# Contiguous-row weight transfers and an earlier first dV in a memory-bound transformer-block backward kernel

## Chip, cores, metric

One core of a Trainium2 chip. The metric is the device time of one execution in microseconds (us), as the median of several executions.

## What is computed

Forward and backward of a decode block: layer norm, attention of one query against a K and V cache, output projection, then layer norm and a gated MLP, and the gradients of everything.

```python
# x (4,1,512), k_cache and v_cache (4,32,4096,128), wq (512,4096), wo (4096,512)
# w1, w3 (512,1792), w2 (1792,512); all bf16
def _A_ref(x, k_cache, v_cache, wq, wo):
    q = heads(x @ wq)
    p = softmax(einsum("bhqd,bhkd->bhqk", q, k_cache) * Dh ** -0.5)
    return merge(einsum("bhqk,bhkd->bhqd", p, v_cache)) @ wo
h  = x + _A_ref(layernorm(x), ...)
h2 = h + (silu(n @ w1) * (n @ w3)) @ w2          # n = layernorm(h)
# reference returns h2 and the gradients of x, k_cache, v_cache, wq, wo, w1, w3, w2
```

K, V, dK and dV are 134 MB each, and V is read twice (once for the output, once for dP). So 705 MB must move and hardly anything else matters: dV of a head is an outer product of the softmax row P and dO, dK one of dS and q.

## The kernel before

The program has three parts: the forward over 128 heads (K and V in, no writes), the **middle** (MLP forward and backward on 4 rows, ending in dO), and the backward over 128 heads (V in, dK and dV out). SBUF is a ring of 23 slots of about 1 MB. Weight loads and weight gradients of the second half are **side work**, cut into pieces by `yield` and fed in between the heads.

```python
    class Slot:                                    # one of 23 buffers [128, 4160] bf16
        def __init__(self, name, src=free):
            self.i = src.popleft()                 # in order of giving back; waits until its last use is done
            ...
    def load_w2():
        sl = two_slots("w2")
        for i in range(2):
            nc.sync.dma_start(out=sl[i].b(7 * D).rearrange("p (c j) -> p c j", c=7),
                              in_=B_w2[i * 7 * P:(i + 1) * 7 * P, :].rearrange("(c p) j -> p c j", p=P))
    ...
    # end of the middle: dO of head 0 of all four batch rows spread to 128 partitions
    ps = psA.tile([P, B, Dh], FP32, tag="rT", name="rep_ps")
    for b in range(B):
        for jj in range(DC):
            nc.tensor.matmul(ps[:, b, :], lhsT=dhT[:, jj, b:b + 1].to_broadcast([P, P]), rhs=wo_page(0)[:, 0, jj, :], ...)
    nc.scalar.copy(out=rep_bufs["rdo"][0], in_=ps[:])
    dO_columns(0, 8, psC, "cols")                  # dO of 8 heads as columns, for dP
    mid_w["wo"][0].give()
    V_T(0, psT, range(2, SJ // GW))                # rest of V of head 0 transposed
    ...
    # side work: second load of wq, by blocks of columns, 2 KB rows
    nc.sync.dma_start(out=wq2s[-1].b(DC * HH * Dh).rearrange("p (c n) -> p c n", c=DC),
                      in_=A_wq[:, ch * HH * Dh:(ch + 1) * HH * Dh].rearrange("(c p) n -> p c n", p=P))
    ...
    # gradient of wo, 1 KB rows (those of w2 likewise)
    nc.gpsimd.dma_start(out=out_5[h0 * P:(h0 + 8) * P, :].rearrange("(h p) j -> p h j", p=P),
                        in_=st.b(8 * D).rearrange("p (h j) -> p h j", h=8))
    ...
    O0, S0 = 2, 18                                 # heads at which dO pages and side work start
    P_pairs(0); P_pairs(1)
    grad_V(0)                                      # outer product on DVE, then a GpSimd DMA
    dO_rows(0, 8, psg, "gps")
    front(0)                                       # transposes V, dP = V dO; P_pairs(s+2) on GpSimd
    for s in range(NH):
        prefetch()
        if s + 1 < NH:
            ...
            front(s + 1)
            grad_V(s + 1)
        grad_K(s)
        ...
```

## Time and profile before

| | before |
|---|---|
| median of 4 runs | 1732.17 us (1729.33 to 1736.33) |
| span of the profiled run | 1729.8 us |
| moved | 707.86 MB, 409 GB/s |
| busy: PE, DVE, ACT, GpSimd | 77%, 72%, 55%, 25% |
| packets of weight reads from SP's queue | 7680 of 1024 bytes, 2048 of 2048, 1024 of 3584 |
| packets of weight writes from GpSimd's queue | 1472 of 4096 bytes, 512 of 7168 |

One thing helps in all that follows: the DMA engines are busy nearly throughout, so progress is best measured in bytes moved, and two traces of this program are best compared at **equal bytes**. I took the packet records of each trace, added up the sizes in order of their ends (without instruction fetches), and noted when 20, 280, 330, 470, 580 and 690 MB had landed. The forward ends near 280 MB, the middle and its after-effects lie at 280 to 330, the weight loads of the second half (wq, then w2) at 470 to 580, the weight gradient writes of w2, w1/w3 and wo at 580 to 690.

### The profile page before, as it was taken

What the parts mean: (1) busy time and instruction counts of PE and PEld (TensorE: products, weight loads), DVE (VectorE), ACT (ScalarE), POOL (GpSimd) and SP (SyncE); (2) the same over time, 40 slices, a digit from 0 to 9 for tenths busy, and PEclk for the clock granted to TensorE, in tenths of its full rate; (3) what the DMA queues carried; (4) which work ended last, traced back from release to release, by engine and by line L of the source; (5) the groups of instructions that cost most, each with busy time, mean ns of one, the idle gap of its engine ahead of it and who ended that gap; (6) DMA issues with size and microseconds to landing.
All of it is one profiled execution on the core that took longest, in us unless ns stands there. A gap on an engine that the chain in (4) does not pass through costs nothing.

```text
span 1729.8 us, 44048 instructions
## 1 busy us (share of the span) xinstructions
PE 1328.0 (77%) x19014; PEld 1121.1 (65%) x19014; DVE 1253.1 (72%) x1388; ACT 959.0 (55%) x1469; POOL 432.5 (25%) x808
## 2 busy tenths in 40 slices
PE   5888888888888888867788777875776867777662
PEld 4667666777666666866677777765654655556562
DVE  5989899889998996576657666665557555555773
ACT  3455445444454444666655555555665767667562
POOL 1211232223222321222212312232123223212331
PEclk8999999999999999666655565556775656555555
DMA  9999999999999999899999999999999999999997
GB/s 399 410 418 418 419 418 419 418 418 417 415 417 408 418 402 391 342 392 424 418 416 412 413 411 414 414 413 418 422 423 421 425 419 411 412 413 411 407 417 294
DMA packets 107179, 707.86 MB, mean 409 GB/s; under 512 B 11284, under 2 KB 18976, under 8 KB 24040
## 3 DMA queue, kind: packets, MB, share of 16 engines
q1 hardware_dynamic: 66880, 422.60, 59.4%
q0 software_dynamic: 39712, 282.37, 39.9%
q8 instruction: 149, 2.44, 0.5%
q14 instruction: 46, 0.38, 0.1%
q10 hardware_dynamic: 392, 0.07, 0.0%
HBM read 422.59 MB, written 282.34 MB: 408 GB/s over the span
## 4 chain that ended last, share of the span: by engine, by line
DMA 38%; PE 8%; ACT 7%; DVE 6%; issue 3%; ACTq 0%; POOL 0%; DVEq 0%; POOLq 0%
DMA out_dram<-gk 22%; DMA out_dram<-gv 9%; ACT VT L760 5%; DMA wq<-in_A_wq_dram 3%; DVE gk L1116 3%; PE pt_tps L759 3%; DVE gv L1116 2%; DMA out_dram<-gwq 2%; DMA out_dram<-gw 1%; PE gps L909 1%; PE M_ps L433 1%; DVE PK L418 1%; PE dP_ps L1110 1%; PE pt_w L562 0%; PE rep_ps L1088 0%
## 5 line engine op out<-in xcount | busy, mean ns | idle before, releaser
L760 ACT COPY VT<-pt_tps 128x1024 bf16<-128x1024 bf16 x512 | 493.1, 1016 | 231.0 <-PE pt_tps L759 122.2
L759 PE MATMUL pt_tps<-ident_b,V 128*128 128x128 bf16 x4096 | 455.2, 294 | 112.7 <-ACT VT L760 98.1
L759 PEld LDWEIGHTS <-V 128*128 128x128 bf16 x4096 | 404.1, 138 | 183.9 <-issue 161.1
L1116 DVE TENSOR_TENSOR gv<-P,reps 128x4096 bf16<-128x4096 bf16 x128 | 293.2, 2291 | 241.2 <-DMA out_dram<-gk 117.5
L1116 DVE TENSOR_TENSOR gk<-dS,reps 128x4096 bf16<-128x4096 bf16 x128 | 293.4, 2292 | 64.4 <-DMA out_dram<-gv 33.0
L433 PE MATMUL M_ps<-PK,Vn 128*128 128x130 bf16 x4096 | 285.7, 222 | 51.5 <-DMA Vn<-in_A_v_cache_dram 50.9
L418 DVE TENSOR_TENSOR PK<-Kn,PK 128x4096 bf16<-128x4096 bf16 x128 | 292.3, 2283 | 32.5 <-POOL PK L414 32.2
L433 PEld LDWEIGHTS <-Vn 128*128 128x128 bf16 x4096 | 252.4, 99 | 73.2 <-DMA Vn<-in_A_v_cache_dram 67.6
L325 DVE STREAM_TRANSPOSE KT<-Kn 128x512 f32<-128x512 f32 (+1 forms) x321 | 250.6, 797 | 0.3 <-issue 0.2
L320 ACT COPY KT<-pt_tps 128x1024 bf16<-128x1024 bf16 x128 | 129.5, 1012 | 193.1 <-PE pt_tps L319 153.1
L1110 PE MATMUL dP_ps<-dOT_bf,VT 128*128 128x1 bf16 x4096 | 152.8, 166 | 67.0 <-ACT VT L760 66.0
L1110 PEld LDWEIGHTS <-VT 128*128 128x128 bf16 x4096 | 140.4, 103 | 79.8 <-ACT VT L760 78.5
L1141 POOL DMA_DIRECT2D out_dram<-gk x128 | 68.1, 532 | 358.5 <-DVE gk L1116 257.5
L1127 POOL DMA_DIRECT2D out_dram<-gv x128 | 68.5, 535 | 322.6 <-DVE dSt L1134 241.7
L331 POOL TENSOR_TENSOR W<-qrep,wmask 128x128 bf16<-128x128 bf16 x128 | 123.9, 968 | 82.2 <-PE S_ps L351 67.4
L414 POOL COPY PK<-P_all 128x64 bf16<-128x64 bf16 x128 | 32.4, 253 | 421.9 <-ACT P_all L408 418.8
L1100 POOL COPY P<-P_all 128x64 bf16<-128x64 bf16 x128 | 112.0, 876 | 0.0
L408 ACT COPY P_all<-pt_P 32x64 bf16<-32x64 bf16 x256 | 51.9, 203 | 59.8 <-PE pt_P L404 57.6
L319 PE MATMUL pt_tps<-ident_b,Kn 128*128 128x128 bf16 x1024 | 80.7, 224 | 0.0
L443 PE MATMUL kP_ps<-PK,onesw 128*32 128x512 bf16 x1024 | 79.2, 386 | 0.0
L319 PEld LDWEIGHTS <-Kn 128*128 128x128 bf16 x1024 | 62.0, 100 | 25.9 <-issue 25.8
L397 ACT ACTIVATE Pn<-E,rl 128x1024 bf16<-128x1024 f32 x64 | 73.7, 1152 | 3.2 <-DVE rl L394 3.2
(228 smaller groups left out, 1294.0 us busy)
## 6 DMA issues: line engine op xcount, KB each, us to landing
Kn<-in_A_k_cache_dram SPq DMA_DIRECT2D x128, 1024.0 KB, 15.6
Vn<-in_A_v_cache_dram SPq DMA_DIRECT2D x128, 1024.0 KB, 16.0
V<-in_A_v_cache_dram SPq DMA_DIRECT2D x128, 1024.0 KB, 11.0
out_dram<-gv POOLq DMA_DIRECT2D x128, 1024.0 KB, 24.6
out_dram<-gk POOLq DMA_DIRECT2D x128, 1024.0 KB, 25.1
wq<-in_A_wq_dram SPq DMA_DIRECT2D x8, 1024.0 KB, 11.2
out_dram<-gw POOLq DMA_DIRECT2D x6, 896.0 KB, 27.4
wo<-in_A_wo_dram SPq DMA_DIRECT2D x4, 1024.0 KB, 13.3
```

Source lines behind the costliest of these rows:

```text
L319: nc.tensor.transpose(pt[:, i, :], Kn[:, c * GW + i, :], ident_b[:])
L320: nc.scalar.copy(out=KT[:, c * GW:(c + 1) * GW, :], in_=pt[:])
L325: nc.vector.transpose(out=KT[:, c * w_:(c + n) * w_], in_=Kn[:, c * w_:(c + n) * w_])
L331: nc.gpsimd.tensor_tensor(out=W[:, hl], in0=qrep[:, :, s:s + 1].to_broadcast([P, 4, 32]), in1=wmask[:, hl, None, :].to_broadcast([P, 4, 32 ...
L418: nc.vector.tensor_tensor(out=PK[:, :, 0:Dh].rearrange("p j (r t) -> p j r t", t=2), in0=Ks[s].heads().rearrange("p j (r t) -> p j r t", t=2),
L433: nc.tensor.matmul(hold["M"][:], lhsT=Vn[:, j, :], rhs=PK[:, j, :], start=(j == 0), stop=(j == SJ - 1))
L443: nc.tensor.matmul(hold["kP"][32 * q:32 * (q + 1), :, :], lhsT=ones_window(w), rhs=PK[:, j0:j0 + 4, 0:Dh], start=(w == 0 and c == 0), stop ...
L759: nc.tensor.transpose(pt[:, i, :], Vn[:, g * GW + i, :], ident_b[:])
L760: nc.scalar.copy(out=VT[:, g * GW:(g + 1) * GW, :], in_=pt[:])
L1100: nc.gpsimd.tensor_copy(out=P2s[s][:], in_=P_all[:, s, :, None].to_broadcast([P, SJ, 2]))
L1110: nc.tensor.matmul(dP_ps[:, j:j + 1], lhsT=VT[:, j, :], rhs=dOT_bf[:, s:s + 1], start=True, stop=True)
L1116: nc.vector.tensor_tensor(out=dst.rearrange("p j (r t) -> p j r t", t=2), in0=col2[:, :, None, :].to_broadcast([P, SJ, Dh // 2, 2]), in1=r ...
```

## The change

Intent: weight rows that one partition holds are made neighbours in HBM, so that a partition's piece is one run of 7 or 8 KB; and the first two dV are made inside the middle, for which dO of one head is spread ahead of the others and q before it, so that writes start sooner. Core of the diff:

```diff
-  in_=B_w2[i * 7 * P:(i + 1) * 7 * P, :].rearrange("(c p) j -> p c j", p=P))
+  in_=B_w2.rearrange("(p c) j -> p c j", c=FC)[:, i * 7:(i + 1) * 7, :])
 ... (the eviction of w2T, hh for o2 and the rows of the gradients are permuted to match)
+        ps = psA.tile([P, REP, Dh], FP32, tag="rT", name="repq_ps")     # q spread, early in the middle
+        ...
+        for s in range(3):
+            P2s[s] = rs.t[...]                                          # pairs of P for three heads, early
+            nc.gpsimd.tensor_copy(out=P2s[s], in_=P_all[:, s, :, None].to_broadcast([P, SJ, 2]))
 ...
+        for b0, b1 in ((0, 1), (1, B)):
+            ps = psA.tile([P, B, Dh], FP32, tag="rT", name="rep_ps")
+            ... (4 matmuls, then 12)
+            if b0 == 0:
+                nc.vector.tensor_copy(out=rep_bufs["rdo"][0][:, 0:1], in_=ps[:, 0:1])
+                grad_V(0)
+            else:
+                nc.scalar.copy(out=rep_bufs["rdo"][0][:, b0:b1], in_=ps[:, b0:b1])
         dO_columns(0, 8, psC, "cols")
         mid_w["wo"][0].give()
+        grad_V(1)
         V_T(0, psT, range(2, SJ // GW))
+        dO_rows(0, 8, psA, "rT")
 ...
-  in_=A_wq[:, ch * HH * Dh:(ch + 1) * HH * Dh].rearrange("(c p) n -> p c n", p=P))
+  nc.sync.dma_start(out=wq2s[-1].b(HD), in_=A_wq[cc * P:(cc + 1) * P, :])
 ... (dx by column blocks; w2 loaded two wq gradients later; o2 after the rows are transposed)
-  nc.gpsimd.dma_start(out=out_5[...].rearrange("(h p) j -> p h j", p=P), ...)
+  nc.gpsimd.dma_start(out=out_5[...].rearrange("(p k) j -> p k j", k=8), ...)   # gw2, gw13 likewise
                 dO_columns(8 * pg, 8 * pg + 8, psg, "gps")
+                yield
                 dO_rows(8 * pg, 8 * pg + 8, psg, "gps")
-        O0, S0 = 2, 18
+        O0, S0 = 2, 21
```

More of the change, by code (lines that the diff above doesn't have):

```diff
@@ L521, in d_hh_units @@
                     nc.tensor.transpose(pt[:, k, :], w2_view(w2, 7 * i + k)[:, jj * P:(jj + 1) * P], ident_b[:])
-                nc.scalar.copy(out=w13_view(w2T, jj)[:, i * 7 * P:(i + 1) * 7 * P].rearrange("p (n c) -> p n c", c=P),
-                               in_=pt[:, 0:7, :])
+                nc.scalar.copy(out=w13_view(w2T, jj).rearrange("q (p c) -> q p c", c=FC)[:, :, i * 7:(i + 1) * 7],
+                               in_=pt[:, 0:7, :].rearrange("q c p -> q p c"))
                 yield
@@ L764, in V_T, with outer, grad_V @@
         (vring if len(V2s) + len(vring) < NV2 else free).append(sl.i)
+    P2s, first_gv = {}, []
+    def outer(dst, col2, row):
+        nc.vector.tensor_tensor(
+            out=dst.rearrange("p j (r t) -> p j r t", t=2),
+            in0=col2[:, :, None, :].to_broadcast([P, SJ, Dh // 2, 2]),
+            in1=row.rearrange("p (r t) -> p r t", t=2)[:, None, :, :].to_broadcast([P, SJ, Dh // 2, 2]),
+            op=ALU.mult,
+        )
+    def grad_V(s):
+        b, h = bh_of(s)
+        gv = Slot("gv")
+        outer(gv.heads(), P2s.pop(s), reps["rdo", s // REP][:, s % REP, :])
+        nc.gpsimd.dma_start(out=rows_of(out_3[b, h]), in_=gv.heads())
+        if s > 1:
+            gv.give()
+        else:
+            first_gv.append(gv)
     NV2 = 6
@@ L857 @@
             load_V2()
+        ps = psA.tile([P, REP, Dh], FP32, tag="rT", name="repq_ps")
+        for i in range(REP):
+            nc.tensor.matmul(ps[:, i, :], lhsT=ident_b[:, i:i + 1].to_broadcast([P, P]), rhs=qrows_bf[:], start=True, stop=True)
+        nc.scalar.copy(out=rep_bufs["rq"][0], in_=ps[:])
+        reps["rq", 0] = rep_bufs["rq"][0]
+        for s in range(3):
+            P2s[s] = rs.t[:, 3840 + 2 * SJ * s:3840 + 2 * SJ * (s + 1)].rearrange("p (j t) -> p j t", t=2)
+            nc.gpsimd.tensor_copy(out=P2s[s], in_=P_all[:, s, :, None].to_broadcast([P, SJ, 2]))
         z = mid.tile([P, 2, DC, B], FP32, name="z")
@@ L876 @@
         nc.gpsimd.tensor_tensor(out=dhT_f[:], in0=u[:], in1=grT[:], op=ALU.add)
-        ps = psA.tile([P, B, Dh], FP32, tag="rT", name="rep_ps")
-        for b in range(B):
-            for jj in range(DC):
-                nc.tensor.matmul(ps[:, b, :], lhsT=dhT[:, jj, b:b + 1].to_broadcast([P, P]), rhs=wo_page(0)[:, 0, jj, :],
-                                 start=(jj == 0), stop=(jj == DC - 1))
-        nc.scalar.copy(out=rep_bufs["rdo"][0], in_=ps[:])
-        reps["rdo", 0] = rep_bufs["rdo"][0]
+        reps["rdo", 0] = rep_bufs["rdo"][0]
+        for b0, b1 in ((0, 1), (1, B)):
+            ps = psA.tile([P, B, Dh], FP32, tag="rT", name="rep_ps")
+            for b in range(b0, b1):
+                for jj in range(DC):
+                    nc.tensor.matmul(ps[:, b, :], lhsT=dhT[:, jj, b:b + 1].to_broadcast([P, P]), rhs=wo_page(0)[:, 0, jj, :],
+                                     start=(jj == 0), stop=(jj == DC - 1))
+            if b0 == 0:
+                nc.vector.tensor_copy(out=rep_bufs["rdo"][0][:, 0:1], in_=ps[:, 0:1])
+                grad_V(0)
+            else:
+                nc.scalar.copy(out=rep_bufs["rdo"][0][:, b0:b1], in_=ps[:, b0:b1])
         dO_columns(0, 8, psC, "cols")
         mid_w["wo"][0].give()
+        grad_V(1)
         V_T(0, psT, range(2, SJ // GW))
+        dO_rows(0, 8, psA, "rT")
     with ExitStack() as c2:
@@ L940, in side_work, with load_wq2 @@
             dx_ps = psx.tile([P, 512], FP32, tag="x2", name="dx_ps")
-            HH = 8
             wq2s = deque()
-            def load_wq2(ch):
+            def load_wq2(cc):
                 wq2s.append(Slot("wq2"))
-                nc.sync.dma_start(out=wq2s[-1].b(DC * HH * Dh).rearrange("p (c n) -> p c n", c=DC),
-                                  in_=A_wq[:, ch * HH * Dh:(ch + 1) * HH * Dh].rearrange("(c p) n -> p c n", p=P))
+                nc.sync.dma_start(out=wq2s[-1].b(HD), in_=A_wq[cc * P:(cc + 1) * P, :])
             load_wq2(0)
@@ L951, in side_work @@
                 yield
-            for ch in range(H // HH):
-                if ch + 1 < H // HH:
-                    load_wq2(ch + 1)
+            wqTv = wqT.b(HD).rearrange("p (n c) -> p n c", c=P)
+            for cc in range(DC):
+                if cc + 1 < DC:
+                    load_wq2(cc + 1)
                 yield
@@ L957, in side_work @@
                 wq2 = wq2s.popleft()
-                wv = wq2.b(DC * HH * Dh).rearrange("p (c n) -> p c n", c=DC)
-                for hl in range(0, HH, 2):
-                    pt = psg.tile([P, 2, DC, P], BF16, tag="gps", name="pt_wq")
-                    for i in range(2):
-                        for cc in range(DC):
-                            nc.tensor.transpose(pt[:, i, cc, :], wv[:, cc, (hl + i) * Dh:(hl + i + 1) * Dh], ident_b[:])
+                for h0 in range(0, H, 8):
+                    pt = psg.tile([P, 8, P], BF16, tag="gps", name="pt_wq")
+                    for i in range(8):
+                        nc.tensor.transpose(pt[:, i, :], wq2.b(HD)[:, (h0 + i) * P:(h0 + i + 1) * P], ident_b[:])
                     yield
-                    nc.scalar.copy(out=wqT.b(HH * D).rearrange("p (n c) -> p n c", c=P)[:, hl * DC:(hl + 2) * DC, :],
-                                   in_=pt.rearrange("p a c k -> p (a c) k"))
+                    nc.scalar.copy(out=wqTv[:, h0:h0 + 8, :], in_=pt[:])
                 wq2.give()
                 yield
-                for hl in range(HH):
-                    h = ch * HH + hl
-                    nc.tensor.matmul(dx_ps[0:B, :], lhsT=dqT_bf[:, h * B:(h + 1) * B], rhs=wqT.b(HH * D)[:, hl * D:(hl + 1) * D],
+                for h in range(H):
+                    nc.tensor.matmul(dx_ps[0:B, cc * P:(cc + 1) * P], lhsT=dqT_bf[:, h * B:(h + 1) * B], rhs=wqTv[:, h, :],
                                      start=(h == 0), stop=(h == H - 1))
+                    if h == H // 2 - 1:
+                        yield
                 yield
@@ L986, in side_work @@
             yield
-            w2 = load_w2()
             for cc in range(DC):
+                if cc == DC - 2:
+                    w2 = load_w2()
                 st = Slot("gwq")
@@ L998, in side_work @@
             fs.give()
-            o2_ps = psx.tile([P, 512], FP32, tag="x2", name="o2_ps")
-            for fc in range(FC):
-                nc.tensor.matmul(o2_ps[0:B, :], lhsT=hhT_bf[:, fc, :], rhs=w2_view(w2, fc), start=(fc == 0), stop=(fc == FC - 1))
-            for sl in w2:
-                sl.give()
-            yield
-            h2_bf = rs.t[0:B, 3328:3328 + D]
-            nc.vector.tensor_tensor(out=h2_bf, in0=hrows, in1=o2_ps[0:B, :], op=ALU.add)
-            nc.gpsimd.dma_start(out=o0_2, in_=h2_bf)
-            yield
             r1, r2 = Slot("rows1"), Slot("rows2")
@@ L1023, in side_work @@
                     nc.scalar.copy(out=dst_rows[:, c0 * P:(c0 + 7) * P].rearrange("b (c f) -> b c f", f=P), in_=pt[:])
+            hhT_p = r2.t[:, 3072:3072 + FC * B].rearrange("p (c b) -> p c b", b=B)
+            pt = psg.tile([P, FC, B], BF16, tag="gps", name="pt_hhp")
+            for fc in range(FC):
+                nc.tensor.transpose(pt[:, fc, :], hh_rows.rearrange("b (p c) -> b c p", c=FC)[:, fc, :], ident_b[0:B, 0:B])
+            yield
+            nc.scalar.copy(out=hhT_p, in_=pt[:])
+            yield
+            o2_ps = psx.tile([P, 512], FP32, tag="x2", name="o2_ps")
+            for fc in range(FC):
+                nc.tensor.matmul(o2_ps[0:B, :], lhsT=hhT_p[:, fc, :], rhs=w2_view(w2, fc), start=(fc == 0), stop=(fc == FC - 1))
+            for sl in w2:
+                sl.give()
+            yield
+            h2_bf = rs.t[0:B, 3328:3328 + D]
+            nc.vector.tensor_tensor(out=h2_bf, in0=hrows, in1=o2_ps[0:B, :], op=ALU.add)
+            nc.gpsimd.dma_start(out=o0_2, in_=h2_bf)
+            yield
             for i in range(2):
                 st = Slot("gw2")
+                hw = hh_rows[:, i * 7 * P:(i + 1) * 7 * P].rearrange("b (p k) -> b k p", k=7)
                 for k in range(7):
-                    fc = 7 * i + k
-                    grad_unit(st.b(7 * D)[:, k * D:(k + 1) * D], hh_rows[:, fc * P:(fc + 1) * P], gr_bf)
+                    grad_unit(st.b(7 * D)[:, k * D:(k + 1) * D], hw[:, k, :], gr_bf)
                     yield
                 grad_flush()
-                nc.gpsimd.dma_start(out=out_8[i * 7 * P:(i + 1) * 7 * P, :].rearrange("(c p) j -> p c j", p=P),
+                nc.gpsimd.dma_start(out=out_8[i * 7 * P:(i + 1) * 7 * P, :].rearrange("(p c) j -> p c j", c=7),
                                   in_=st.b(7 * D).rearrange("p (c j) -> p c j", c=7))
@@ L1039, in side_work @@
                     st = Slot("gw13")
+                    nw = hhat_bf[0:B, i * 2 * P:(i + 1) * 2 * P].rearrange("b (p k) -> b k p", k=2)
                     for k in range(2):
@@ L1042, in side_work @@
                             grad_unit(st.b(2 * F)[:, k * F + f0_:k * F + f0_ + w_],
-                                      hhat_bf[0:B, (2 * i + k) * P:(2 * i + k + 1) * P], rows[:, f0_:f0_ + w_])
+                                      nw[:, k, :], rows[:, f0_:f0_ + w_])
                             yield
                     grad_flush()
-                    nc.gpsimd.dma_start(out=out_ap[i * 2 * P:(i + 1) * 2 * P, :].rearrange("(c p) f -> p c f", p=P),
+                    nc.gpsimd.dma_start(out=out_ap[i * 2 * P:(i + 1) * 2 * P, :].rearrange("(p c) f -> p c f", c=2),
                                       in_=st.b(2 * F).rearrange("p (c f) -> p c f", c=2))
@@ L1051, in side_work @@
                 st = Slot("gwo")
+                ow = oflat.b(HD)[0:B, h0 * P:(h0 + 8) * P].rearrange("b (p k) -> b k p", k=8)
                 for k in range(8):
-                    h = h0 + k
-                    grad_unit(st.b(8 * D)[:, k * D:(k + 1) * D], oflat.b(HD)[0:B, h * P:(h + 1) * P], dh_bf)
+                    grad_unit(st.b(8 * D)[:, k * D:(k + 1) * D], ow[:, k, :], dh_bf)
                     yield
                 grad_flush()
-                nc.gpsimd.dma_start(out=out_5[h0 * P:(h0 + 8) * P, :].rearrange("(h p) j -> p h j", p=P),
-                                  in_=st.b(8 * D).rearrange("p (h j) -> p h j", h=8))
+                nc.gpsimd.dma_start(out=out_5[h0 * P:(h0 + 8) * P, :].rearrange("(p k) j -> p k j", k=8),
+                                  in_=st.b(8 * D).rearrange("p (k j) -> p k j", k=8))
                 st.give()
@@ L1071, in rest_of_dO @@
                 dO_columns(8 * pg, 8 * pg + 8, psg, "gps")
+                yield
                 dO_rows(8 * pg, 8 * pg + 8, psg, "gps")
@@ L1092, in replicate @@
                 reps[nm_, i0 // REP] = rt
-        bwd, P2s = {}, {}
+        bwd = {}
         def P_pairs(s):
-            if s < NH:
+            if s < NH and s not in P2s:
                 P2s[s] = bw3.tile([P, SJ, 2], BF16, tag="P2", name="P2")
@@ L1113, in front @@
             bwd[s] = dP_ps
-        def outer(dst, col2, row):
-            nc.vector.tensor_tensor(
-                out=dst.rearrange("p j (r t) -> p j r t", t=2),
-                in0=col2[:, :, None, :].to_broadcast([P, SJ, Dh // 2, 2]),
-                in1=row.rearrange("p (r t) -> p r t", t=2)[:, None, :, :].to_broadcast([P, SJ, Dh // 2, 2]),
-                op=ALU.mult,
-            )
-        def grad_V(s):
-            b, h = bh_of(s)
-            gv = Slot("gv")
-            outer(gv.heads(), P2s.pop(s), reps["rdo", s // REP][:, s % REP, :])
-            nc.gpsimd.dma_start(out=rows_of(out_3[b, h]), in_=gv.heads())
-            gv.give()
         def grad_K(s):
@@ L1146, in prefetch @@
                 load_V2()
-        O0, S0 = 2, 18
-        P_pairs(0)
-        P_pairs(1)
-        grad_V(0)
-        dO_rows(0, 8, psg, "gps")
+        O0, S0 = 2, 21
         front(0)
@@ L1159 @@
                     load_V2()
+                if s == 0:
+                    V_T(1, psT)
+                    first_gv[0].give()
                 front(s + 1)
-                grad_V(s + 1)
+                if s > 0:
+                    grad_V(s + 1)
             grad_K(s)
+            if s == 0:
+                first_gv[1].give()
             if s >= S0:
-                step("s", 1 if s < S0 + 44 else 3)
+                step("s", 1 if s < S0 + 38 else 3)
             elif s >= O0:
```

## The prediction

> **What bounds the kernel now.** I read the page's header and its row of 40 slices first, then the chain that ended last, then tables of stretches of 10 us and 1 us, then the timeline of the one stretch that looked different.
>
> ```profile
> PE 1328.0 (77%) x19014; PEld 1121.1 (65%) x19014; DVE 1253.1 (72%) x1388; ACT 959.0 (55%) x1469; POOL 432.5 (25%) x808
> ...
> DMA  9999999999999999899999999999999999999997
> GB/s 399 410 418 418 419 418 419 418 418 417 415 417 408 418 402 391 342 392 424 418 416 412 413 411 414 414 413 418 422 423 421 425 419 411 412 413 411 407 417 294
> DMA packets 107179, 707.86 MB, mean 409 GB/s; under 512 B 11284, under 2 KB 18976, under 8 KB 24040
> ...
> DMA 38%; PE 8%; ACT 7%; DVE 6%; issue 3%; ACTq 0%; POOL 0%; DVEq 0%; POOLq 0%
> ```
>
> The reader is to see that no compute engine is full, while the 16 DMA engines are at nine tenths or more in all slices but one in the middle and the last, at a rate near 419 GB/s. The chain agrees: its largest item is DMA, mostly dK and dV leaving (out_dram<-gk 22%, gv 9%). A kernel like this can win only three things: DMA time lost to small packets, stretches where the DMA engines stand idle, and the drain at the end. The ceiling of all three together: 707.86 MB at 419 GB/s take 1689 us, the span is 1729.8, so about 40 us (2.3%) are lost altogether. Adding up (1 - rate/419) over stretches of 10 us says where: about 13 us in the last 20 us, 2 at the start, 3 at 660 to 680, 11 in the middle between 700 and 780; the rest is spread thinly.
>
> ```profile
> 690.00:700.00 10.00, 9.89 (x175) 9.77 (x173) 5.68 (x17) 7.93 (x11) 0.00 (x0) 0.68 1.01 420
> 700.00:710.00 10.00, 7.96 (x180) 7.71 (x177) 4.19 (x12) 4.70 (x6) 0.57 (x3) 0.83 0.78 310
> 710.00:720.00 10.00, 9.02 (x124) 8.21 (x124) 8.09 (x10) 6.22 (x8) 6.19 (x8) 0.51 0.69 280
> 720.00:730.00 10.00, 8.51 (x122) 7.69 (x120) 7.01 (x5) 6.95 (x8) 3.62 (x6) 0.50 0.99 332
> ...
> 770.00:780.00 10.00, 7.67 (x128) 6.88 (x125) 8.59 (x9) 7.56 (x9) 5.07 (x6) 0.75 1.00 344
> ...
> 1710.00:1720.00 10.00, 0.00 (x0) 0.00 (x0) 0.00 (x0) 0.00 (x0) 0.00 (x0) 0.50 0.67 283
> 1720.00:1730.00 10.00, 0.00 (x0) 0.00 (x0) 0.00 (x0) 0.00 (x0) 0.00 (x0) 0.50 0.04 17
> ```
>
> The last two columns are the DMA share and GB/s. At 700 to 720 engines are really idle (0.78, 0.69). At 720 to 730 and 770 to 780 they are counted as busy but slow (332 and 344 GB/s): in the packet records one V load of 128 packets of 8192 bytes averages 515 ns a packet at 724 to 728 and one 506 ns at 772 to 776, where 311 ns is the median. At the end the compute engines have nothing left and the last writes drain.
>
> Why the middle is idle, from its timeline (start, us, engine, line):
>
> ```profile
> 704.42 0.18 DVE L875 TENSOR_TENSOR dhT<-u,grT 128x16 bf16<-128x16 f32 x1
> ...
> 704.74 1.91 PE L881 MATMUL rep_ps<-wo,dhT 128*128 128x128 bf16 x16
> ...
> 706.69 0.59 ACT L883 CAST reps<-rep_ps 128x512 bf16<-128x512 f32 x1 [0.59 <-PE rep_ps L881]
> ...
> 707.82 2.28 DVE L1116 TENSOR_TENSOR gv<-P,reps 128x4096 bf16<-128x4096 bf16 x1
> ...
> 710.40 0.62 POOL L1127 DMA_DIRECT2D out_dram<-gv  x1 [5.36 <-DVE gv L1116]
> ...
> 714.73 2.29 DVE L1116 TENSOR_TENSOR gk<-dS,reps 128x4096 bf16<-128x4096 bf16 x1 [1.04 <-DMA out_dram<-gv]
> ...
> 717.32 0.53 POOL L1141 DMA_DIRECT2D out_dram<-gk  x1 [3.21 <-DVE gk L1116]
> ```
>
> All free buffers hold V loads already, so reads run dry at 706, and nothing can be written before the first dV exists. From dhT (704.6) it takes 16 matmuls, an eviction of four heads on ACT and two small DVE operations of the dO columns before the first dV starts at 707.82. Its transfer is issued at 710.40, the second dV's at 713.56, the first dK's at 717.32.
>
> **What the Trainium skill says.** Three places bear on it. "DMA: Bandwidth & Descriptors", section "Where 436 GB/s comes from", gives 435 GB/s for the fabric and about 358 for one core's part of the HBM; the trace has 418 to 424 over most of the span, so here the first is the ceiling in sight. The same page, "Why small descriptors are slow (HBM only)", names a fixed cost for each packet. The trace agrees: read packets of 8192 bytes have a median of 311 ns, of 2048 bytes 84 ns, of 1024 bytes 46 ns, where an eighth of 311 is 39. The same page, "SWDGE vs HWDGE vs iDMA", says that packets are up to 4096 bytes preferably. In the trace only the writes from GpSimd's queue join 1024-byte rows so: there are 1472 packets of 4096 bytes, just the bytes of the gw2 and gwo writes (6.03 MB), while the same rows read from SP's queue go as 1024 bytes each. So the writes have little to win from contiguous rows.
>
> **The change part by part. Contiguous rows.** The packet records of the trace, grouped by queue and size, give each cost as engine time over 16 engines. The w2 loads (two, one in each half) are 3584 packets of 1024 bytes, mean 50.4 ns in the first and 46.1 in the second: 172.9 us of engine time, 10.8 us of span. After, 512 packets of 7168 bytes; for these I take the 283 ns mean of the 7168-byte packets that are already written: 9.1 us. Saved 1.7. The second wq load: 2048 packets at 84.35 ns are 10.8 us, after 512 of 8192 bytes at 315.9 ns 10.1. Saved 0.7. The gw2 and gwo writes: 1472 packets of 4096 bytes at 170.7 ns are 15.7 us, after 256 of 7168 at 283 and 512 of 8192 at 319 14.7. Saved 1.0. The w1/w3 gradients go as 512 packets of 7168 bytes already, so nothing. All these run where the DMA share is 1.0, so they count in full: 3.4 us. The wo, w1 and w3 loads at 660 to 690 are untouched. The counter-cost is strided operands: an eviction of w2T with a step of 14 elements (8 times), row weights with a step. These lie on ACT (55% busy) and PE, beside the DMA.
>
> **The middle.** The change removes from the way to the first dV 12 of its 16 matmuls (1.91 us down to about 0.5), replaces ACT's 0.59 us by a DVE copy of one head (about 0.2, like the other small copies there), and moves the two dO column operations behind it. The first dV then starts at about 704.6 + 0.1 + 0.5 + 0.3 = 705.6 and is issued at 708.1, where it was 710.4: 2.3 us earlier. The second dV follows after two small operations, 708.4 to 710.7, issued at about 710.9, where it was 713.6. The dK waited 1.04 us for a dV's buffer; the order of give-backs now hands it the buffer of the transposed V, and its dP no longer waits for the spreading of q, so I put it at 712, issued at 714.4, where it was 717.3. The DMA engines' idle time between 702 and 720 adds up, from the 1 us table, to 5.6 us:
>
> ```profile
> 709.00:710.00 1.00, 0.07 (x1) 0.00 (x0) 1.00 (x1) 0.88 (x1) 0.00 (x0) 1.00 0.32 123
> 710.00:711.00 1.00, 1.00 (x7) 0.82 (x6) 0.30 (x3) 0.25 (x1) 0.60 (x1) 0.56 0.02 8
> ...
> 714.00:715.00 1.00, 0.85 (x8) 0.84 (x8) 0.27 (x1) 1.00 (x2) 0.11 (x1) 0.50 0.41 164
> ...
> 717.00:718.00 1.00, 0.81 (x14) 0.82 (x15) 1.00 (x2) 0.13 (x1) 0.68 (x2) 0.50 0.11 33
> ```
>
> With writes starting at about 709, of 2.5 us each, every 3 us, I get 1.6 us idle before the first, 0.3 and 0.9 between the next, some 2.7 in all. Saved 3 us. The hole at 768 (0.74 us, the next page of dO) is eased by a yield between columns and rows: 0.3 us. Side work starts three heads later and ends about one head later (the last weight gradient is issued at 1627.8 now, and 13 heads follow), so the drain is the same.
>
> Sum: 3.4 + 3 + 0.3 = 6.7 us, 1733.7 - 6.7 = 1727.
>
> **The rivals.** First, the time won in the middle is not lasting: V loads and writes share the 16 engines, so an earlier write may only shift reads, and the pace afterwards could be set by the ACT copies of transposed V (1016 ns, four a head, the chain's 5%). For it: ACT copies and matmuls stand in the chain between 803 and 850. Against: the DMA share is 1.0 there, so idle time filled is bytes moved. It would leave 1730. Second, a slow stretch like the two V loads at 515 ns goes away or is doubled, since the mixture of reads and writes in the middle is another: plus or minus 1.7 us each. Third, the larger read packets hold other queues up, or wq loads now wait for a different buffer: the old ones took up to 39 us to land, with SP's queue of V loads behind them. It would show as DMA share under 1 at 1180 to 1300, and cost a few us. Fourth, long drains at the end: single engines run on from 1716 to 1726; where they end is partly luck, plus or minus 3 us.
>
> **Range and chances.** 1727 is the sum; the second and fourth rivals and the scatter of runs (1730.66 to 1736.33) give some 5 us either way, and I leave more room below, as the smaller packet counts may also smooth neighbours: 1717 to 1733. Faster by over 2% means under 1699, nearly the whole 40 us: 2%. Slower by over 2% would need 35 us of new idle DMA: 1%.
>
> **What would show it.** Right: no 2048-byte packets and 3584 fewer of 1024 bytes, so that the count under 2 KB falls by 3584; the first dV issued near 708; the idle sum of the middle near 2.7 us; the other slices unchanged at 412 to 424 GB/s. Wrong, if the first dV is earlier and the end is not, if w2 and wq were not in full stretches, or if the share drops below 1 in a stretch that was full.

## The result, and the profile after

| | before | after |
|---|---|---|
| median | 1732.17 us (4 runs) | 1725.28 us (4 runs, 1723.44 to 1726.79) |
| span of the profiled run | 1729.8 us | 1721.7 us |

The ratio is 0.9958, with a 95% interval of 0.9933 to 0.9982. (Ratios are the mean time of one kernel's runs over that of the other's of the same rounds, so not quite the ratio of the medians quoted.) That is 6.9 us between the medians, where 6.7 was predicted. The page of the changed kernel, the lines that answer to those in the prediction:

```profile
PE 1330.3 (77%) x19124; PEld 1129.6 (66%) x19124; DVE 1253.5 (73%) x1389; ACT 960.7 (56%) x1470; POOL 422.6 (25%) x808
...
GB/s 398 418 419 418 419 418 419 418 413 419 417 417 405 419 403 390 373 419 420 418 415 411 416 410 410 412 417 419 423 417 413 419 417 414 418 416 414 414 417 314
DMA packets 101868, 707.88 MB, mean 411 GB/s; under 512 B 11284, under 2 KB 15392, under 8 KB 17704
...
DMA 47%; DVE 6%; PE 4%; issue 3%; ACT 2%; POOL 0%; POOLq 0%; DVEq 0%; ACTq 0%
```

The slices of the middle went from 342 and 392 GB/s to 373 and 419. The packets under 2 KB fell by 18976 - 15392 = 3584, just as predicted. The bound is the same, with less of PE and ACT in the chain. The stretches of 10 us in the middle (last two columns: DMA share, GB/s):

```profile
700.00:710.00 10.00, 8.88 (x184) 8.27 (x180) 6.56 (x14) 5.05 (x7) 1.43 (x5) 0.78 0.82 332
710.00:720.00 10.00, 8.80 (x119) 8.29 (x120) 9.19 (x9) 7.01 (x8) 6.88 (x8) 0.53 0.92 378
720.00:730.00 10.00, 7.24 (x106) 6.29 (x103) 5.07 (x5) 6.67 (x8) 2.27 (x4) 0.64 1.01 347
...
770.00:780.00 10.00, 7.35 (x88) 6.81 (x88) 6.76 (x8) 6.44 (x8) 1.84 (x4) 0.50 1.01 419
```

The shares of 700 to 720 rose from 0.78 and 0.69 to 0.82 and 0.92; the slow stretch at 770 is gone, the one at 720 is not: the V load there averages 442 ns a packet instead of 515. Summing the missing shares of 702 to 720 from the 1 us table gives 2.7 us idle in this trace, as predicted, where it was 5.6 (not every run has this: see the end of the experiments). The timeline of the changed kernel's middle:

```profile
703.61 0.18 DVE L904 TENSOR_TENSOR dhT<-u,grT 128x16 bf16<-128x16 f32 x1
...
704.69 0.29 DVE L915 CAST reps<-rep_ps 128x128 bf16<-128x128 f32 x1 [0.90 <-PE rep_ps L912]
705.11 2.29 DVE L769 TENSOR_TENSOR gv<-reps 128x4096 bf16<-128x4096 bf16 x1
...
707.70 0.63 POOL L780 DMA_DIRECT2D out_dram<-gv  x1 [3.82 <-DVE dOT_bf L735]
...
710.75 2.29 DVE L769 TENSOR_TENSOR gk<-dS,reps 128x4096 bf16<-128x4096 bf16 x1
...
713.05 0.23 POOL L1143 COPY P<-P_all 128x64 bf16<-128x64 bf16 x1
...
713.34 0.53 POOL L1169 DMA_DIRECT2D out_dram<-gk  x1
```

From the end of dhT to the issue of the first dV it was 5.8 us (704.60 to 710.40) and is now 3.9 (703.79 to 707.70); to the first dK's issue 12.7 and now 9.6.

So far all looks as foretold. At equal bytes it does not: of the 6.3 us that this trace leads at 700 MB, 5.5 were won at 280 to 330 MB and almost nothing by the rows of the second half. That was the reason to take the change apart.

### The profile page after: what moved, and what is told of

Same layout as the page of the kernel before. It is cut to its first block, busy times and chain, and to the rows that moved or that the text cites. A ratio compares the mean times of both kernels' runs of the same rounds, so it can differ in the third digit from the quotient of the medians. Undisturbed runs are those within 1.5% of the kernel's fastest.

```text
span 1721.7 us, 44266 instructions
## 1 busy us (share of the span) xinstructions
PE 1330.3 (77%) x19124; PEld 1129.6 (66%) x19124; DVE 1253.5 (73%) x1389; ACT 960.7 (56%) x1470; POOL 422.6 (25%) x808
## 2 busy tenths in 40 slices
DMA packets 101868, 707.88 MB, mean 411 GB/s; under 512 B 11284, under 2 KB 15392, under 8 KB 17704
## 4 chain that ended last, share of the span: by engine, by line
DMA 47%; DVE 6%; PE 4%; issue 3%; ACT 2%; POOL 0%; POOLq 0%; DVEq 0%; ACTq 0%
DMA out_dram<-gk 29%; DMA out_dram<-gv 14%; DVE gk L769 3%; DVE gv L769 2%; DMA out_dram<-gwq 2%; DMA out_dram<-gw 2%; ACT VT L760 1%; PE pt_tps L759 1%; PE M_ps L433 1%; DVE PK L418 1%; PE pt_w L562 0%; PE pt_wo L571 0%; ACT Pn L397 0%; POOL P L1143 0%; PE kP_ps L443 0%
## 5 line engine op out<-in xcount | busy, mean ns | idle before, releaser
L769 DVE TENSOR_TENSOR gv<-P,reps 128x4096 bf16<-128x4096 bf16 x125 | 286.5, 2292 | 233.9 <-DMA out_dram<-gk 131.2
L1143 POOL COPY P<-P_all 128x64 bf16<-128x64 bf16 x125 | 103.6, 829 | 0.0
## 6 DMA issues: line engine op xcount, KB each, us to landing
wq<-in_A_wq_dram SPq DMA_DIRECT2D x8, 1024.0 KB, 13.2
```

Source lines behind the costliest of these rows:

```text
L769: nc.vector.tensor_tensor(out=dst.rearrange("p j (r t) -> p j r t", t=2), in0=col2[:, :, None, :].to_broadcast([P, SJ, Dh // 2, 2]), in1=r ...
L1143: nc.gpsimd.tensor_copy(out=P2s[s][:], in_=P_all[:, s, :, None].to_broadcast([P, SJ, 2]))
```

## The experiments

Each group of runs ran on one chip with its own runs of the kernel before: the first four runs below in one, small_loads to mid_look2 in another, the last four in a third. All results were correct. Two theories stood at the start: **A**, the prediction's, that packet time counts in full wherever the DMA share is 1.0; **B**, that the middle alone is the gain.

### rows_only: only the contiguous rows

```diff
  (the kernel before, with the hunks for w2, the second wq, gw2, gw13, gwo, o2)
-        O0, S0 = 2, 18
+        O0, S0 = 2, 21        # and 38 single steps instead of 44, as in the change
```

> The kernel before with only the contiguous rows (loads of w2 and second wq, writes of gw2, w1/w3 and wo gradients, with the later start of side work that they came with). Theory A (packets count in full, as predicted): 3.4 us faster than before, ratio 0.998, the lead over before growing by about 0.9 us at the first w2 load and by 2.5 us in the second half. Theory B (the middle is the change, as the lead of the two traces hints: 5.6 of some 6.3 us): ratio 0.9995, lead 0.8 us at the first w2 load and then nearly flat.

Measured: 1728.1 us (1726.95 to 1730.11), ratio 0.9972 (0.9954 to 0.9991). Theory A's size, and theory B's 0.9995 lies outside the interval.

### mid_only: only the middle

```diff
  (the kernel before, with the hunks for repq_ps, P2s, rep_ps in two parts, grad_V(0), grad_V(1), dO_rows, the yield)
-        O0, S0 = 2, 18
+        O0, S0 = 2, 21        # the pause between columns and rows needs three more steps
```

> The kernel before with only the earlier first two dV, the spreading of one head first, q ahead, and the pause between dO columns and rows (with the start of side work at head 21 that this pause needs). Theory A: 3.3 us faster, ratio 0.998. Theory B: 5.5 us faster, ratio 0.9968, first dV issued near 708, and the hole at 768 gone.

Measured: 1737.52 us (1730.81 to 1743.88), ratio 1.0024 (0.9996 to 1.0051). Neither theory: no gain at all, and runs that lie 13 us apart. Its profile, of the fastest run, has the first dV at 709.02 (3.98 us after dhT) and a middle stretch 2.2 us shorter than that of before.

### after_again: the changed kernel beside its parts

> The changed kernel again beside the parts on the same chip. Both theories: ratio 0.996, and the two parts' gains add up to its gain within 2 us; if they don't, the parts touch each other.

Measured: 1725.86 us (1724.4 to 1728.1), ratio 0.9959 (0.9940 to 0.9978). The parts' gains (3.9 and minus 5.5) don't add up to 6.2, so they touch each other, or something else comes in with the old rows.

### v2_1k: the packet cost blown up

```diff
-  nc.sync.dma_start(out=V2s[s].heads(), in_=cache_head(A_v_cache, s))
+  nc.sync.dma_start(out=V2s[s].t[:].rearrange("p (a c) -> p a c", c=520)[:, :, 0:512],
+                    in_=cache_head(A_v_cache, s).rearrange("p (a j) d -> p a (j d)", a=8))
   (the transposes read the padded rows)
```

> The changed kernel with the suspected packet cost blown up: the 128 V loads of the second half go in runs of 1024 bytes (1024 packets a load instead of 128), same bytes. If packet time counts in full: 1024 packets of 46 to 50 ns less 128 of 315 ns, over 16 engines, is 0.43 to 0.70 us a load, 55 to 90 us in all, ratio to before 1.028 to 1.048. If the packet times of the records overlap or the writes beside them hide the cost: under 25 us.

Measured: 1772.75 us, ratio 1.0232 (1.0205 to 1.0259): 46.9 us over the changed kernel of the same chip, 0.37 us a load. The 1024-byte packets averaged 49.0 ns, so their time alone foretold (1024 x 49.0 - 128 x 315.5) / 16 = 0.61 us a load, 78 us: 60% of it showed, which lies between the two expectations. The records overlap: with small packets the packet times of a full stretch add up to 1.03 to 1.05 of it, where they add up to 1.01 otherwise. So packet time is real, but in this run it counted in part. What the loads lose here they also take from V: in the waits of PE in the second half,

```profile
PE pt_tps L760 <- DMA V<-in_A_v_cache_dram: 137.9, 19, 14.1
```

138 us in 19 waits. From this came theory **C**: the two queues take turns. The Trainium skill, "DMA: Bandwidth & Descriptors", section "Queues, rings and completion order", says that each DMA engine goes round the queues with work a packet at a time. The packet records of the kernel before agree in kind. Where V loads and writes both have 8192-byte packets, reads to writes come as 209 to 217 GB/s (10 us from 1330) and 177 to 244 (from 1340); at 1300 to 1310, where reads are w2's 1024-byte packets, reads get 71 GB/s beside 339 of writes, and no V load behind them moves at all. (One to one by records would be 1 to 8; it is 1 to 4.8. By that section a packet can hold several descriptors, so a record of the trace need not be one turn.) V loads landed after at most 51.0 us, and 19.6 in the changed kernel. If that starved the backward, it would explain why the middle alone gains nothing.

### small_loads and small_stores: packet sizes alone, by padding

In the changed kernel rows of a partition are kept apart in SBUF by 8 or 16 elements, so that HBM addresses and order stay and only the packets shrink.

```diff
  small_loads:
-  load_w2()                                                # the second one
+  load_w2(D + 8)                                           # 1024-byte runs
-  nc.sync.dma_start(out=wq2s[-1].b(HD), in_=A_wq[cc * P:(cc + 1) * P, :])
+  nc.sync.dma_start(out=wq2s[-1].t[:].rearrange("p (a c) -> p a c", c=1040)[:, :, 0:1024], ...)   # 2048-byte runs
  small_stores:
-  grad_unit(st.b(8 * D)[:, k * D:(k + 1) * D], ow[:, k, :], dh_bf)
+  grad_unit(st.t[:, k * 520:k * 520 + D], ow[:, k, :], dh_bf)          # gw2 likewise
```

> The changed kernel with only the packets of its second-half weight loads put back to their old sizes: wq in runs of 2048 bytes and the second w2 in runs of 1024, by padding the rows in SBUF; the rows themselves and all else stay. Theory A (packet time alone): 1.5 us slower than the changed kernel, same scatter. Theory C (new: packets of both queues take turns, so a read in small packets beside writes of 8192 bytes gets a fifth of the engines, and the V loads that stand behind it in the same queue come late): over 5 us slower in the median, a scatter of over 8 us as in the middle alone, V loads landing after up to 45 us where it is 20, PE waiting for V over 10 us.

> The changed kernel with only the writes of the w2 and wo gradients in runs of 1024 bytes again. Theory A: packets of 4096 bytes again on the GpSimd queue, 1 us slower. Theory C: the same, since these packets are big enough and no load stands behind them; no added scatter. If the time is over 4 us worse, the stores are the cause.

Measured: small_loads 1725.74 us (1723.11 to 1727.62), ratio 0.9958 (0.9944 to 0.9972); small_stores 1729.32 us (1728.03 to 1730.71), ratio 0.9983 (0.9971 to 0.9995).

Both theories missed. With small load packets V landed after up to 46.0 us and PE waited 16.5 us for it, and yet the time is that of the changed kernel: theory C falls, as far as the median goes. The lines of V, small_loads first, then the changed kernel:

```profile
  DMA V<-in_A_v_cache_dram: 16.5, 5
DMA to landing us min/median/max: 8.2/10.9/46.0
...
DMA to landing us min/median/max: 8.8/10.7/19.6
```

The write packets, which theory A put at 1 us, show as 3.6 us between small_stores and small_loads. (The changed kernel was not run on this chip; small_loads has the same ratio to before as after_again.)

### mid_look1 and mid_look2: the middle alone

> A second look at the middle alone, whose six runs went from 1730.8 to 1743.9 us while its profile was of the fastest. In two of three looks a slow run should be caught. Theory C: the longer it is, the longer PE waited for V behind the wq and w2 loads, and lead is lost between 470 and 600 MB. Rival: the time is lost evenly, in slower packets all over the second half.

> The same once more, for the chance of a slow run; as for the look before.

Measured: 1728.78 and 1732.27 us, on the second chip. No slow run was caught, so they say nothing of its cause ("slow" is used from here on for the long runs of the scatter, over 1735 us, a line drawn after seeing them); they do show that the middle alone can be quick.

### small_both, mid_again

small_both has the edits of small_loads and small_stores together; mid_again is mid_only once more.

> The changed kernel with both the second-half weight loads and the weight gradient writes in small packets, by padded rows. Theory D (new: the stretches of equal bytes add up; the loads' packets cost nothing there, small ones were even 1.7 us quicker, and small write packets cost 2.7 us): ratio to before 0.9975, 1727.5 us, stretch 470 to 580 MB 262.5 us, 580 to 690 MB 268.2 us, scatter like the changed kernel's. Theory E (small loads and small writes together bring the scatter seen in the first job): median over 1731, single runs over 1736.

> The middle alone once more with rounds, as its first six runs had a median of 1737.5 and two later looks on another chip 1728.8 and 1732.3. Theory D: the gain of the middle stretch shows, ratio 0.9985, 1729.5 us, and the slow runs belonged to that chip or hour. Theory E: median over 1734 again.

Measured: small_both 1727.42 us (1723.96 to 1728.68), ratio 0.9968 (0.9945 to 0.9990), as theory **D** has it, and without slow runs. mid_again 1730.49 us (1725.27 to 1744.36), ratio 1.0002 (0.9969 to 1.0035): theory D put the scatter down to the first chip or hour, and here it is on a third chip. This time the profile is of a slow run, 1736.92 us. Its lost time is in one place; stretches of 10 us, and three waits on the way there (PE, ACT, DVE):

```profile
1380.00:1390.00 10.00, 5.78 (x75) 5.28 (x74) 0.92 (x3) 6.48 (x8) 1.84 (x4) 0.50 0.96 368
1390.00:1400.00 10.00, 7.74 (x89) 6.03 (x88) 7.28 (x7) 7.32 (x9) 1.42 (x4) 0.67 0.75 272
```

```profile
1331.78 1.89 PE L759 MATMUL pt_tps<-ident_b,V 128*128 128x128 bf16 x16 [13.00 <-DMA V<-in_A_v_cache_dram]
...
1382.80 0.90 ACT L1059 COPY rows<-pt_Tr 4x896 bf16<-4x896 bf16 x1 [4.94 <-issue]
...
1387.12 0.53 DVE L1051 TENSOR_SCALAR rows<-rows_t,mv_h,rstd_h 4x512 bf16<-4x512 f32 x1 [7.08 <-DMA out_dram<-gwq]
```

PE stands 13.0 us for a V load that was queued behind the w2 load. 50 us later the side work takes two slots for small rows whose last content, a gradient of wq, is still on its way out: DVE stands 7.08 us for that transfer (ACT 4.94, for which the profile names nothing), and in program order no dV and no dK are made, and now the DMA engines run dry (0.75). At equal bytes the stretch of 470 to 580 MB took 269.0 us, 6 us over the others of its kind. DVE stands 4.7 to 7.7 us before that instruction in each of the 13 traces other than v2_1k's (the profile names a gwq transfer in nine), and in the 12 besides this one the DMA share stays at 0.98 or more in every stretch of 10 us from 1360 to 1420, so work still queued covers it. That the two meet is shown for this one run only.

### dv_halves, spread_all

```diff
  dv_halves: outer() and the transfer of the first dV in two halves of 16 rows a partition
  spread_all:
-  for b0, b1 in ((0, 1), (1, B)):
+  for b0, b1 in ((0, B),):                        # all four spread, evicted on ACT, then grad_V(0)
```

> The changed kernel with the very first dV made and sent in two halves, an attempt at a better version: the first transfer is issued half an outer product (1.15 us) earlier, at about 706.6, and the DMA engines' idle time before the first write shrinks by about as much. By the theory that an idle engine filled counts in full: 1 us faster than the changed kernel, ratio to before 0.9955. By the rival that it only shifts work: no change in the stretch of 280 to 330 MB.

> The changed kernel with dO of all four heads spread before the first dV, one look for its issue times. By the prediction's working, the 12 other matmuls and the ACT eviction come back: first dV issued about 1.5 to 2 us later than 707.7, near 709.5, and second near 712.

Measured: dv_halves 1725.18 us (1724.07 to 1726.38), ratio 0.9959 (0.9940 to 0.9978): no better version within what can be told apart. From dhT to the first issue it took 2.90 us instead of 3.91, as planned, but its middle stretch was 126.9 us, like after_again's. That is what the rival expected (work only shifted), but one trace can't tell 1 us where those of this middle spread from 125.0 to 129.1. spread_all, one look at 1728.82 us, issued the first dV at 708.82, 5.33 us after dhT: 1.4 us of the lead comes from spreading one head first.

The look at issue times showed a wait that nobody had foretold. In after_again, GpSimd and DVE around the first dK, then the DMA share per us:

```profile
710.50 2.34 POOL L746 CAST dOT_f<-dOT_bf 128x32 f32<-128x32 bf16 x1
712.78 2.29 POOL L1143 COPY P<-P_all 128x64 bf16<-128x64 bf16 x1
715.02 0.53 POOL L1169 DMA_DIRECT2D out_dram<-gk  x1
```

```profile
710.48 2.29 DVE L769 TENSOR_TENSOR gk<-dS,reps 128x4096 bf16<-128x4096 bf16 x1
712.68 2.30 DVE L769 TENSOR_TENSOR gv<-reps 128x4096 bf16<-128x4096 bf16 x1
```

```profile
713.00:714.00 1.00, 1.00 (x28) 1.00 (x26) 1.00 (x1) 1.00 (x2) 1.00 (x1) 0.50 0.77 311
714.00:715.00 1.00, 0.51 (x18) 0.43 (x16) 0.98 (x1) 0.63 (x1) 1.00 (x1) 0.50 0.16 57
715.00:716.00 1.00, 1.00 (x14) 1.00 (x11) 0.78 (x3) 0.03 (x1) 1.00 (x4) 0.50 0.00 0
```

The dK is ready at 712.77 and is issued at 715.02, since GpSimd, which issues it, is in a copy of 128x64 that takes 0.24 us at its shortest (median 0.42 in this trace) and here lasts as long as DVE's outer product (2.29). The Trainium skill, "SBUF — State Buffer", section "SBUF: two separate sides", says that DVE and GpSimd share a pair of ports as an exclusive lock, held for a whole instruction, also where a DVE instruction with two inputs in SBUF meets a GpSimd one that reads SBUF, as here; the trace agrees (0.24 against 2.29 us). The DMA engines are idle for 2 us for it. In the first trace of the changed kernel the same copy came at 713.05, just ahead of DVE's next outer product, and took 0.23: the dK left at 713.34. Nine traces have this middle unaltered. In seven the copy is held (2.29 to 2.37 us) ahead of the first dK's issue: idle sums of 4.1 to 5.7 us between 702 and 720, and 126.4 to 129.1 us at equal bytes. In two, after and small_both, it is not: 2.7 us idle, and 125.0 and 126.1. Making that copy after the dK's issue, or on another engine, was not tried.

## The traces at equal bytes

Time in us for each stretch, from the packet records of every profile (the last column runs from 690 MB to the last packet; "new" and "old" are rows and packets as after and as before):

| kernel | 20-280 MB | 280-330 | 330-470 | 470-580 | 580-690 | 690-end |
|---|---|---|---|---|---|---|
| before | 631.3 | 130.5 | 339.1 | 261.8 | 268.2 | 44.3 |
| rows_only | 630.3 | 130.1 | 338.2 | 264.1 | 264.6 | 43.7 |
| mid_only | 631.2 | 128.3 | 338.2 | 262.9 | 268.4 | 45.3 |
| mid_look1, mid_look2 | 631.2, 631.4 | 127.6, 129.1 | 338.7, 338.9 | 262.8, 263.8 | 268.1, 267.9 | 43.8, 44.6 |
| mid_again (slow run) | 631.3 | 126.4 | 338.5 | 269.0 | 267.2 | 48.0 |
| after, after_again | 630.7, 630.3 | 125.0, 126.9 | 339.7, 338.8 | 263.8, 264.3 | 265.7, 265.6 | 42.6, 44.2 |
| small_loads | 630.4 | 128.2 | 338.4 | 261.7 | 266.0 | 47.0 |
| small_stores | 630.5 | 128.5 | 337.7 | 264.8 | 268.4 | 44.3 |
| small_both | 630.3 | 126.1 | 338.0 | 262.2 | 267.9 | 46.1 |
| dv_halves, spread_all | 631.0, 630.3 | 126.9, 128.7 | 338.5, 338.3 | 264.6, 265.3 | 267.2, 266.7 | 42.4, 43.6 |

Means over the table: the first w2 load in large packets saves 0.8 us; the new middle 2.9 (127.4 against 130.3); large load packets **cost** 2.0 in their stretch (264.5 against 262.5, the slow run left out); large write packets save 2.0 (266.0 against 268.0). The last stretch is 1.7 shorter with large load packets (43.5 against 45.2, the slow run left out), so what they cost before is nearly given back there.

The slow runs are the other half of the story. Over all jobs, 7 of 37 runs of the kernel before and 5 of 14 of the middle alone took over 1735 us, up to 1744; of the 41 runs of kernels with the new rows, small packets or large, none took over 1730.8 (v2_1k left out). The packets of the second-half loads are hardly what removes them: the 12 runs of small_loads and small_both have none. For loads and writes together there are only the six of small_both, which at the rate of the middle alone would all be quick by chance about once in 14. What is left are the order of the side work (w2 loaded two gradients later, o2 moved), the rows' addresses in HBM and the first w2 load, which is in large packets in small_both too; no run tells these apart. Without the runs over 1735 us the means are 1731.4 us before (30 runs), 1730.4 for the middle alone (9), 1728.4 for the rows alone (6) and 1725.7 for the changed kernel (10): then each part gains, 1.0 and 3.0 us, and both together 5.7.

## Why the prediction was right, and where it was not

**The bound and the ceiling**: right. DMA share and rate are the same, and no version came near 2%.

**The first w2 load** (1.1 us of the 1.7 for w2, by the prediction's own means of 50.4 and 46.1 ns): 0.8 at equal bytes. Right in mechanism, a little smaller in size.

**The middle** (3 us, and 0.3 for the hole at 768): right in direction and size, 2.9 us at equal bytes, and 2.2 between rows_only and after_again. The hole at 768 is gone (DMA share at 760 to 770 0.91 before, 1.01 after). The issue times were foretold well. Counted from the end of dhT, which came 0.8 us earlier in the trace after, the first dV was put at 3.5 us and seen at 3.9, the second at 6.3 and 6.4, the first dK at 9.8 and 9.6. That the idle sum is 2.7 as foretold was luck of the trace: in seven of nine the GpSimd copy, which the prediction missed, leaves 4.1 to 5.7, little less than the 5.6 of before. Those seven still gain 2.4 us (mean 127.9): 1.3 is time in which engines are less idle, and 1.1 is packets that took less time (their sum over 16 engines is 123.5 us against 124.6). The prediction had the second kind only as its rival of slow V loads. The first rival (time only shifted) is refuted: with the new middle the stretch of 330 to 470 MB is as long as without (337.7 to 339.7 against 338.2 and 339.1), so the lead stays.

**The second-half loads** (1.3 us by the prediction's means: 0.6 for w2, 0.7 for wq; small_loads was expected at 1.5): wrong. "All these run where the DMA share is 1.0, so they count in full" is the step that failed. In time nothing is gained (small_loads 0.9958 against 0.9959 for after_again, each by its own chip's before); in their stretch 2.0 us are lost, and the last stretch gives 1.7 back. The packet records show how they are lost: the reads of the stretch take 1.5 us less of all 16 engines (means of 90.3 against 91.9), but the writes beside them go from a mean of 313 ns to 318, and 8800 of them make 2.7 us; the records also overlap 0.7 us less. Why writes are longer beside large reads, and why the last stretch is shorter, is open.

**The gradient writes** (1.0 us): the mechanism was right, the term mis-sized: 2.0 us at equal bytes. By run times it is 3.6 between small_stores and small_loads, but only 0.0010 in ratio, 1.7 us, between small_both and small_loads. The packets themselves save the 1.0 (15.7 to 14.7 us); the rest are their neighbours. From before to the changed kernel the 8143 other writes in the stretch go from a mean of 323 ns to 319 or 320. Where padding alone differs, neither these writes (318 to 321 ns with large gradient writes, 321 in small_stores; 316 in small_loads and in small_both) nor the reads (311 to 318 against 317; 319 against 325) show it clearly, so which neighbours pay is open.

**The drain**: "the same", plus or minus 3. The last stretch is 42.4 to 44.3 us with large load packets and 43.8 to 47.0 with small ones, so not the same, but inside that bound.

**Not in the prediction**: that a slower group of runs goes with the old rows. The predicted 6.7 met the measured 6.9 partly because the terms that failed are of opposite sign, and partly because medians of before hold some slow runs: without these the gain is 5.7, and the stretches add up to 5.4 (0.8 + 2.9 - 2.0 + 2.0 + 1.7). So the closeness of the sum is luck. The second rival came in part: of the two slow V loads one is gone (419 GB/s at 770) and one went from 515 to 442 ns. The third rival looked for trouble with wq's large packets; it was the old small ones that landed late (39.2 us, now 16.3 at most).

## What to carry to other kernels

Where DMA engines are full, compare traces at equal bytes moved, and take packet times as a rough guide only: 78 us of them counted as 46.9, 1.3 as nothing and 1.0 as 2.0, since a packet's neighbours changed by more than the packet saved. A part tried alone (here the middle, 1.0024 and 1.0002) can look worthless because of scatter that is absent when another part is in, so look at single runs and not only at the median. In a program whose transfers are issued by a compute engine, check what that engine does just before each issue.

## What the Trainium skill lacked or had wrong

- "DMA: Bandwidth & Descriptors", "Queues, rings and completion order": it has packets as the turn between queues, but not what that makes of unequal ones. Here 1024-byte reads got 71 GB/s beside 339 of 8192-byte writes (1 to 4.8, not 1 to 8), and V loads behind them in the same queue landed after up to 51 us instead of 19.6.
- "DMA: Bandwidth & Descriptors", "Why small descriptors are slow (HBM only)": has a cost for each packet, but no page says how much of a profile's packet times shows in the end (v2_1k, 46.9 us of 78), or that packets of one queue lengthen those of the other: writes of 8192 bytes averaged 313 ns beside small reads and 318 beside large ones.
- "SBUF — State Buffer", "SBUF: two separate sides": has the lock for just this pair of instructions, and agrees (0.24 us against 2.29). What it tells of held transfers is about writing their descriptors; here a plain small copy ahead of the issue in GpSimd's program order held a transfer for 2.25 us.
- No page has the slow loads of V in the middle: 515, 506 and 442 ns a packet in three loads after 13.8, 7.3 and 13.2 us of writes alone, where 311 is the median. The writes alone are not the reason: in the changed kernel's trace a load after 8.6 us of them averaged 310 ns, and after_again's after 12.7 us 323. The cause is open.
